# S4 convolution and SwiGLU on one core: half of the spectra paired by VectorE, the direct term on VectorE, block 1's halves kept on chip

## The chip, the core and the metric

The kernel runs on one core of one Trainium2 chip. The core has TensorE (matrix products into PSUM), VectorE, ScalarE and GpSimd (elementwise work; GpSimd also issues one kind of transfer) and SyncE, which issues most transfers here. Each engine works through its own instructions in a fixed order and waits for others at semaphores. The metric is the device time of one execution in microseconds (us), median of the runs. A profile is one further execution.

## The reference

Four residual layers on `x` of 2048 rows (L) by 512 columns (D): an S4 convolution, a SwiGLU, and both again with the same weights.

```python
dt = jnp.exp(log_dt)[:, None]
logdA = dt * A                      # A complex, D x N, N = 128
P = jnp.exp(logdA[:, :, None] * l)  # l = 0..2047
K = jnp.einsum("dn,dnl,dn->dl", Cc, P, dB).real
y = irfft(rfft(u, 2 * L) * rfft(K, 2 * L))[:L] + u * Dskip
...
x = x + A_ref(layernorm(x)); x = x + B_ref(layernorm(x))   # twice
B_ref(x) = (silu(x @ w_gate) * (x @ w_up)) @ w_down
```

K has 2048 lags for each of the 512 columns, and does not depend on x, so the kernel makes it once and uses it in both convolution layers.

## The kernel before

Two stages follow one another. The first, up to about 340 us, **builds** the spectra of K; the second runs the convolutions and the SwiGLU. The change is in the first.

The build runs over 8 chunks (`NCH`) of 64 columns (`DC`), and chunk c's steps are spread over two periods. In the order of data:

- **Tables of chunk c + 2** (`gen_turns`, `gen_exp`, `gen_trig`): VectorE makes phases in `im` (lines 386, 390 and the four doublings of line 394), ScalarE turns them into sines and cosines (lines 406 to 408) and makes the powers (line 421).
- **Factors of chunk c + 1** (`gen_g`, `gen_e`): VectorE multiplies them up (lines 441 to 448 into `re` and `im`; lines 455 to 483 into `g`, where the last half of `g` is completed by a 1 MB adding transfer that GpSimd issues, line 473).
- **Lags** (`lags`, lines 493 and 494): 128 small TensorE products from `g`, `re` and `im` give the chunk's 2048 x 64 lags in PSUM, `pk`. They need the last of VectorE's factors (line 448).
- **Spread** (`spread_in`, `spread`): ScalarE copies `pk` to `ks` (line 504); SyncE stores it to DRAM (`kdr`, line 511) and loads it back in another arrangement with four transfers (`kt`, line 513). For chunk 6 TensorE rearranges it instead (line 520), with a ScalarE copy (line 522).
- **Direct term** (`skip`, line 500): `Dskip` is added to lag 0, one row of `kt`, 1 x 64 elements. GpSimd does it for chunks 0 to 6; chunk 7's is VectorE's.
- **Spectra** (`spectra`): TensorE multiplies `kt` by the Fourier matrices (line 528) into `pw` in PSUM, for the frequency residues `q0` and `q0 + 2`: a call with q0 = 0 for chunks 0 to 6 and one with q0 = 1 for chunks 0 to 5, the latter a period later. The result W for three block offsets is the sum of two halves, one of block k and one, with a sign and real and imaginary parts exchanged, of block k - 1. ScalarE copies one half to `wo` (for q0 = 1 to a part of `spare`), line 552, the other to `wa`, line 554, and block 0 to `w0r`, line 555. SyncE stores `wo` to DRAM (`wdr`, line 535), and GpSimd then issues adding transfers of `wa` onto the same places (line 535 too, called from line 561): the pairing is done by the transfers. `wa` has one buffer.
- **Block 1's direct transform** (`second`, `direct`, lines 302 and 290): a half h and a residue q per chunk. SyncE loads the half's 512 rows from DRAM (`ndr`) into two buffers of the tag `uu` (line 306; the tag has three), TensorE transforms them (line 296), ScalarE copies the result (line 299), and SyncE stores it (line 300). Four residues use the same half, and each loads it again.
- **Norms of the weights** (`norms`): GpSimd loads weight tiles (line 324), ScalarE squares them (line 330), TensorE sums the squares (line 333), VectorE takes the largest (line 336).

The order of the work in the build is written out by hand: each step is put into `plan` with a time (`at(t, step)`), the plan is sorted, and every engine's instructions follow that sequence. The times are only keys of the order; when something runs is settled by the semaphores. `use(c, t)` puts chunk c's steps, `prepare` the tables, `factors` the factors. In the second stage the order is made by a scheduler that simulates the program; a change of the build can therefore move instructions there too.

Of the kernel before, what the change touches and what calls it, by code (L numbers as in the profile page):

```python
# [15 lines left out]
AF = mybir.ActivationFunctionType  # L16
OP = mybir.AluOpType
# [5 lines left out]
P = 128  # L23
T = 512
NB = L // T
FT = 11
FR = F % P
HD = D // 2
# [6 lines left out]
DC = 64  # L35
# [39 lines left out]
def kernel(ctx, tc, x, a_re, a_im, b_re, b_im, c_re, c_im, log_dt, d_skip,  # L75
                           w_gate, w_up, w_down, c_ef, c_ei, c_ek, c_am, c_eh, c_eih, out):
    nc = tc.nc
    V, A, G, PE = nc.vector, nc.scalar, nc.gpsimd, nc.tensor
# [9 lines left out]
    def tl(shape, name, tag, dt=F32):  # L88
        return sb.tile(shape, dt, name=name, tag=tag, bufs=BUFS[tag])
# [58 lines left out]
    ndr = dram.tile([2, 2, P, 2, HD], F32, name="ndr")  # L148
# [141 lines left out]
    def direct(b, h, q, n, space=psml):  # L290

        pf = space([P, 2, HD], "pf")
        for i in range(2):
            for c in range(4):
                e = ek[q // 2][:, q % 2, c - 1, i] if c else ef[:, q, i]
                PE.matmul(pf[:, i], lhsT=e, rhs=n[c], start=c == 0, stop=c == 3)
        yield
        u = tl([P, NQ, 2, DC], "u", "uu")
        A.activation(parted(u), whole(pf), AF.Copy)
        nc.sync.dma_start(udr[0][b, h, q], u)  # L300

    def second(h, q, space=psml):
        n = []
        for cp in range(2):
            t = tl([P, 2, HD], "n1", "uu")
            nc.sync.dma_start(t, ndr[h, cp])
            n += [t[:, 0], t[:, 1]]
        return direct(1, h, q, n, space)


    def norms():
# [185 lines left out]
    def skip(ch, kt, eng):  # L497

        k = kt[0:1, :, 0]
        eng.tensor_tensor(k, k, dsk[:, ch * DC:(ch + 1) * DC].rearrange("p (g d) -> p g d", g=4), OP.add)  # L500
# [33 lines left out]
    def store_w(h, c, q, wo, eng=nc.sync, **add):  # L534
        eng.dma_start(wdr[1:, h, q, :, c].rearrange("k p i d -> p k (i d)"), wo.rearrange("p k i d -> p k (i d)"), **add)

    def spectra(ch, kt, q0):


        h, cq = ch // NQ, ch % NQ  # L540
        pw = pbig([P, 2, 2, NB, 4, 16], "pw")
        for j in range(2):
            products(pw[:, j], kt, 0, NB, q0 + 2 * j, [(i, c) for i in range(2) for c in range(4)])
        yield
        if q0:
            wo = spare[0][:, 16 * DC:].rearrange("p (j k i d) -> p j k i d", j=2, k=NB - 1, i=2)
        else:
            wo = tl([P, 2, NB - 1, 2, DC], "wo", "sg")
        wa = tl([P, 2, NB - 1, 2, DC], "wa", "z")
        pv = pw.rearrange("p j i k g d -> p i j k (g d)")  # L550
        for i, sign in signs(q0):
            A.activation(wo[:, :, :, i], pv[:, 1 - i, :, :NB - 1], AF.Copy, scale=sign)
        for i in range(2):
            A.activation(wa[:, :, :, i], pv[:, i, :, 1:], AF.Copy)
        A.activation(w0r[:, h, q0::2, cq], pw[:, :, :, 0].rearrange("p j i g d -> p j i (g d)"), AF.Copy)
        yield
        for j in range(2):
            store_w(h, cq, q0 + 2 * j, wo[:, j])
        yield
        for j in range(2):  # L560
            store_w(h, cq, q0 + 2 * j, wa[:, j], G, accum_op=OP.add)
        yield

    def first_parts(c0, q):

# [376 lines left out]
    with tc.manual_schedule(engines={mybir.EngineType.Activation, mybir.EngineType.DVE, mybir.EngineType.PE, mybir.EngineType.Pool}):  # L942
# [57 lines left out]
        def at(t, f, n=1):  # L1000
            plan.append((t, len(plan), (lambda: take(f, n)) if hasattr(f, "__next__") else f))
# [5 lines left out]
        def prepare(c, t):  # L1007

            def tiles():
                ts[c] = gen_tiles(c)  # L1010
            at(t + 0.05, tiles)
            steps = {k: later(lambda g=g: g(c, ts[c])) for k, g in
                     (("turns", gen_turns), ("exp", gen_exp))}
            tr = later(lambda: gen_trig(ts[c]))
            at(t + 0.35, steps["turns"])
            at(t + 0.45, tr)
            at(t + 13.0, steps["turns"], 6)
            at(t + 17.0, tr)
            at(t + 8.3, steps["exp"], 100)

# [19 lines left out]
        def use(c, t):  # L1040

            box, kt, n = {}, kt2[:, c % 2], starts[c + 1]

            def copy():
                box["ks"] = spread_in(box["pk"])
                if c < NCH - 2:
                    spread(c, box["ks"], kt)
            at(t, lambda: box.update(pk=lags(ts[c], gs[c])))
            at(t + 7.1, copy)
            if c == NCH - 2:  # L1050
                at(t + 10.0, lambda: spread_pe(box["ks"], kt))
            at(t + 12.5, lambda: skip(c, kt, G))
            at(t + 25.0, lambda: sizes(c, kt, box["ks"]))
            for q0, ats in list(enumerate(((t + 17.5, t + 25.2, n + 2.1, n + 7.5),
                                      (n + 6.9, n + 14.0, n + 17.3, n + 21.0))))[:2 if c < NCH - 2 else 1]:
                sp = later(lambda q0=q0: spectra(c, kt, q0))
                for t0 in ats:
                    at(t0, sp)
# [26 lines left out]
        for i in range(NCH - 1):  # L1085
            t = starts[i]
# [12 lines left out]
        t = starts[NCH - 1]  # L1099
# [8 lines left out]
        c, kts, tail = NCH - 1, (kt2[:, 0], kt2[:, 1]), {}  # L1108
# [149 lines left out]
```

## Time and profile before

| | |
|---|---|
| median of 3 runs | 1203.43 us (1202.81 to 1205.57) |
| the profiled execution | 1196.63 us |
| its span, first to last instruction | 1194.8 us |
| its mean TensorE clock | 0.981 of full |
| busy over the span: TensorE, VectorE, ScalarE, GpSimd | 93%, 83%, 50%, 11% |
| moved by transfers | 156.28 MB in 134643 packets |

In the lines of the profile, PE is TensorE, PEld its weight loads, DVE VectorE, ACT ScalarE, POOL GpSimd, SP SyncE; a "q" behind a name is that engine's sequencer, which issues transfers and waits. L500 is line 500 of the kernel before. A timeline row has the start, the duration (both us), the engine, the line, the operation, output<-input, and the shapes; in brackets stands how long the engine was idle before it and what ended that. Names keep no buffer numbers.

### The profile page before, as it was taken

The page shows a single profiled execution, that of the slowest core. Times are in us where ns is not written, and L with a number is a line of the kernel's source. Part 1 is how long each engine was busy: PE and PEld are TensorE (multiplying, and loading weights), DVE is VectorE, ACT ScalarE, POOL GpSimd, SP SyncE. Part 2 cuts the span into 40 slices and gives each one's busy share as a digit, 9 for nine tenths or more (in the row PEclk, how much of TensorE's full clock was granted, in tenths as well). Part 3 has the DMA queues.
Part 4 walks back from the last instruction along what each step waited for, and adds up shares of the span by engine and source line. Part 5 has one row for each costly group of instructions (what it writes and reads, how often), then busy time and mean ns, then how long its engine had stood idle before and what let it go on. Part 6 is the DMA issues. An engine that isn't in the chain of part 4 may idle for free.

```text
span 1194.8 us, 24454 instructions
## 1 busy us (share of the span) xinstructions
PE 1109.1 (93%) x9948; PEld 880.3 (74%) x9948; DVE 995.7 (83%) x1579; ACT 600.0 (50%) x1208; POOL 132.7 (11%) x183
## 2 busy tenths in 40 slices
PE   1889978898799998999999999989999999999998
PEld 1768867787687676878777686858687786867875
DVE  7999988874888999999899999989996799983211
ACT  6789778833272444447644252664532552325211
POOL 0013333331000010000100000121100010000000
PEclk9989988999899999999999999999999999999999
DMA  5359887879475326433334454433435145312000
GB/s 202 132 149 219 188 165 162 190 178 249 138 228 163 121 101 203 138 120 81 102 96 155 119 163 153 117 90 110 127 124 184 34 121 140 112 58 45 14 23 18
DMA packets 134643, 156.28 MB, mean 131 GB/s; under 512 B 51313, under 2 KB 81777, under 8 KB 134530
## 3 DMA queue, kind: packets, MB, share of 16 engines
q1 hardware_dynamic: 117026, 126.47, 34.4%
q0 software_dynamic: 17504, 28.25, 11.6%
q8 instruction: 78, 1.28, 0.4%
q14 instruction: 35, 0.29, 0.1%
HBM read 101.85 MB, written 36.57 MB: 116 GB/s over the span
## 4 chain that ended last, share of the span: by engine, by line
PE 33%; DVE 22%; issue 9%; DMA 6%; POOL 1%; SPq 1%; ACT 1%; DVEq 0%; POOLq 0%; ACTq 0%
PE pgu L900 5%; PE pgu L901 5%; PE pgu L903 5%; DVE t L767 3%; PE py L915 3%; PE py L916 3%; PE py L917 3%; DVE yk L770 3%; PE pi L787 2%; DVE yk L767 2%; DMA mix<-nn 2%; DVE z L228 2%; PE pf L280 2%; DVE sg L907 1%; DMA w<-wdr 1%
## 5 line engine op out<-in xcount | busy, mean ns | idle before, releaser
L900 PE MATMUL pgu<-mix,wsl 128*128 128x256 f16 x1280 | 298.4, 272 | 5.8 <-DVE xg L920 3.5
L901 PE MATMUL pgu<-mix,wsl 128*128 128x256 f16 x1280 | 298.5, 273 | 0.0
L903 PE MATMUL pgu<-mix,wsl 128*128 128x256 f16 x1280 | 194.8, 273 | 0.0
L901 PEld LDWEIGHTS <-wsl 128*128 128x128 f16 x1280 | 125.2, 98 | 22.8 <-issue 6.9
L915 PE MATMUL py<-wsl,hh 128*128 128x512 f16 (+1 forms) x352 | 134.8, 383 | 6.9 <-DVE xg L920 6.4
L900 PEld LDWEIGHTS <-wsl 128*128 128x128 f16 x1280 | 125.2, 98 | 15.7
L903 PEld LDWEIGHTS <-wsl 128*128 128x128 f16 x1280 | 125.2, 98 | 14.6
L917 PE MATMUL py<-wsl,hl 128*128 128x512 f16 (+1 forms) x352 | 134.7, 383 | 1.0 <-DVE hl L909 1.0
L916 PE MATMUL py<-wsl,hh 128*128 128x512 f16 x320 | 122.7, 383 | 0.0
L767 DVE TENSOR_TENSOR t<-uu,w 128x1024 f32<-128x1024 f32 x96 | 117.1, 1220 | 4.9 <-DMA w<-wdr 4.2
L770 DVE TENSOR_TENSOR yk<-yk,t 128x1024 f32<-128x1024 f32 x96 | 117.1, 1220 | 0.2
L906 ACT ACTIVATE sg<-pgu,sc 128x512 f32<-128x512 f32 x80 | 54.6, 682 | 119.4 <-PE pgu L903 116.2
L907 DVE SCALAR_TENSOR_TENSOR sg<-pgu,sc,sg 128x512 f32<-128x512 f32 x80 | 59.8, 747 | 54.4 <-ACT sg L906 54.3
L528 PE MATMUL pw<-kt,ek 128*128 128x256 f32 (+1 forms) x384 | 96.7, 391 | 0.0
L908 ACT ACTIVATE hh<-sg 128x512 f16<-128x512 f32 x80 | 50.1, 626 | 79.7 <-DVE sg L907 79.7
L528 PEld LDWEIGHTS pw<-kt,ek 128*128 128x128 f32 x384 | 77.1, 205 | 10.5
L787 PE MATMUL pi<-yl,mix 128*128 128x256 f16 x576 | 78.8, 272 | 3.5 <-DVE yl L228 3.3
L280 PE MATMUL pf<-z,eh 128*128 128x256 f16 x576 | 74.9, 273 | 0.1
L767 DVE TENSOR_TENSOR yk<-u,w0r 128x1024 f32<-128x1024 f32 x56 | 68.3, 1220 | 2.8 <-ACT u L282 2.6
L916 PEld LDWEIGHTS <-hh 128*128 128x128 f16 (+1 forms) x352 | 34.7, 99 | 44.5 <-issue 9.4
L909 DVE TENSOR_TENSOR hl<-sg,hh 128x512 f16<-128x512 f32 x80 | 55.0, 688 | 14.8 <-ACT hh L908 14.8
L493 PE MATMUL pk<-re,g 128*32 128x64 f32 x1024 | 61.5, 301 | 5.5 <-DVE re L448 3.3
(237 smaller groups left out, 2186.7 us busy)
## 6 DMA issues: line engine op xcount, KB each, us to landing
w<-wdr SPq DMA_DIRECT2D x96, 256.0 KB, 2.7
uu<-udr SPq DMA_DIRECT2D x96, 256.0 KB, 2.9
udr<-u POOLq DMA_DIRECT2D x32, 256.0 KB, 2.4
g<-g POOLq DMA_DIRECT2D x6, 1024.0 KB, 9.8
wdr<-wa POOLq DMA_DIRECT2D x26, 192.0 KB, 7.0
udr<-u SPq DMA_DIRECT2D x16, 256.0 KB, 3.0
n<-ndr SPq DMA_DIRECT2D x16, 256.0 KB, 4.6
n<-xdr SPq DMA_DIRECT2D x4, 1024.0 KB, 5.7
```

The source lines that it names most:

```text
L280: PE.matmul(pf[:, o], lhsT=e, rhs=m, start=k == 0, stop=k == len(terms) - 1)
L528: PE.matmul(pw[:, i], lhsT=e, rhs=kt[:, :, c + 4 * k0:4 * k1:4, :].rearrange("p g k d -> p k g d"), start=c == 0, stop=c == 3)
L767: V.tensor_tensor(t, uu.unsqueeze(2).to_broadcast([P, NQ, 2, 2, DC]), w.unsqueeze(3).to_broadcast([P, NQ, 2, 2, DC]), OP.mult)
L770: V.tensor_tensor(yk, yk, t, OP.add)
L787: PE.matmul(pi[:, o], lhsT=e, rhs=m, start=k == 0, stop=k == len(terms) - 1)
L900: PE.matmul(o, lhsT=wgu(wi, k, 0)[:, fs], rhs=nh[:, k], start=k == 0, stop=False)
L901: PE.matmul(o, lhsT=wgu(wi, k, 1)[:, fs], rhs=nh[:, k], start=False, stop=False)
L903: PE.matmul(o, lhsT=wgu(wi, k, 0)[:, fs], rhs=nlo[:, k], start=False, stop=k == 3)
L907: V.scalar_tensor_tensor(sg, pgu[:, 1], sc6[:, 4:5], sg, OP.mult, OP.mult)
L915: PE.matmul(py[:, r], lhsT=hh[:n, f, rc], rhs=wd(f, 0)[:n], start=f == 0, stop=False)
L916: PE.matmul(py[:, r], lhsT=hh[:n, f, rc], rhs=wd(f, 1)[:n], start=False, stop=False)
L917: PE.matmul(py[:, r], lhsT=hl[:n, f, rc], rhs=wd(f, 0)[:n], start=False, stop=f == FT - 1)
```

## The change

It has three parts, and a small shift of the order.

- In `spectra`, the calls with q0 = 0 no longer copy the second half to `wa`. VectorE adds it, straight out of PSUM, onto `wo` in place, and SyncE stores the finished sum. The adding transfers remain for q0 = 1.
- `skip` runs on VectorE for all chunks, and stands between the second and the third doubling of the phases (the doublings are split 3 and 3 for it).
- `second` loads a half of block 1 once and keeps its two tiles for the four residues that use it: 4 loads in place of 16. Two of the three buffers of `uu` are taken meanwhile.

```diff
+    halves = {}
+
     def second(h, q, space=psml):
-        n = []
-        for cp in range(2):
-            t = tl([P, 2, HD], "n1", "uu")
-            nc.sync.dma_start(t, ndr[h, cp])
-            n += [t[:, 0], t[:, 1]]
-        return direct(1, h, q, n, space)
+        if h not in halves:
+            halves[h] = n = []
+            for cp in range(2):
+                t = tl([P, 2, HD], "n1", "uu")
+                nc.sync.dma_start(t, ndr[h, cp])
+                n += [t[:, 0], t[:, 1]]
+        return direct(1, h, q, halves[h], space)
...
-        wa = tl([P, 2, NB - 1, 2, DC], "wa", "z")
         pv = pw.rearrange("p j i k g d -> p i j k (g d)")
         for i, sign in signs(q0):
             A.activation(wo[:, :, :, i], pv[:, 1 - i, :, :NB - 1], AF.Copy, scale=sign)
-        for i in range(2):
-            A.activation(wa[:, :, :, i], pv[:, i, :, 1:], AF.Copy)
+        if q0:
+            wa = tl([P, 2, NB - 1, 2, DC], "wa", "z")
+            for i in range(2):
+                A.activation(wa[:, :, :, i], pv[:, i, :, 1:], AF.Copy)
         A.activation(w0r[:, h, q0::2, cq], pw[:, :, :, 0].rearrange("p j i g d -> p j i (g d)"), AF.Copy)
         yield
+        if not q0:
+            wv = wo.rearrange("p j k i d -> p i j k d")
+            V.tensor_tensor(wv, pv[:, :, :, 1:], wv, OP.add)
+            yield
         for j in range(2):
             store_w(h, cq, q0 + 2 * j, wo[:, j])
         yield
-        for j in range(2):
-            store_w(h, cq, q0 + 2 * j, wa[:, j], G, accum_op=OP.add)
-        yield
+        if q0:
+            for j in range(2):
+                store_w(h, cq, q0 + 2 * j, wa[:, j], G, accum_op=OP.add)
+            yield
...
-            at(t + 13.0, steps["turns"], 6)
+            at(t + 13.0, steps["turns"], 3)
+            at(t + 13.2, steps["turns"], 3)
...
-            at(t + 12.5, lambda: skip(c, kt, G))
+            at(t + 13.1, lambda: skip(c, kt, V))
```

What the orders look like at three places, taken from chunk 3's period (line numbers behind each L are those of the kernel that the rows are from; the changed kernel's are 3 to 9 higher).

On VectorE, the place between the factors `g` of one chunk and the factors `re` and `im` of the same chunk, with the doublings of a later chunk's phases between. Before:

```order
L390 TENSOR_TENSOR im<-tdk,am 128x128
L394 ISA im<-im 128x256
L394 ISA im<-im 128x512
L394 ISA im<-im 128x1024
L394 ISA im<-im 128x2048
L443 TENSOR_TENSOR re<-re 128x2048
L445 SCALAR_TENSOR_TENSOR im<-im,mu 128x1984
L448 TENSOR_TENSOR re<-re,mu 128x124x8 x2
```

And in the changed kernel:

```order
L393 TENSOR_TENSOR im<-tdk,am 128x128
L397 ISA im<-im 128x256
L397 ISA im<-im 128x512
L503 TENSOR_TENSOR kt_438<-kt_438,tdk 1x4x16
L397 ISA im<-im 128x1024
L397 ISA im<-im 128x2048
L446 TENSOR_TENSOR re<-re 128x2048
L448 SCALAR_TENSOR_TENSOR im<-im,mu 128x1984
L451 TENSOR_TENSOR re<-re,mu 128x124x8 x2
```

The direct term has come in between the doublings, and everything below it on VectorE now stands behind a wait for `kt`.

On VectorE again, some instructions later, where the next factors `g` begin; the changed kernel alone (before, the row of `wo` is not there):

```order
L458 TENSOR_TENSOR xz<-xz,mz_156 128x960
L462 TENSOR_TENSOR g<-w_152,re 128x2x64
L463 TENSOR_TENSOR spare<-w_152,im 128x2x64
L444 TENSOR_TENSOR im<-im,re 128x2048
L389 TENSOR_TENSOR xz<-th,am 128x320
L563 TENSOR_TENSOR wo<-pw,wo 128x2x6x64
L465 TENSOR_TENSOR g<-g,spare 128x64
L466 TENSOR_TENSOR g<-g,spare 128x64
```

The pairing of q0 = 0, 768 elements a partition, is a new instruction there. It waits for ScalarE's copies to `wo`.

On GpSimd, one period, before:

```order
L396 MEMSET im 128x64
L324 DMA st<-in_B_w_gate_dram 128x344 x3
L535 DMA wdr<-wa 128x3x128 x2
L324 DMA st<-in_B_w_gate_dram 128x344 x2
L535 DMA wdr<-wa 128x3x128 x2
L419 MEMSET re 128x64
L473 DMA g<-g 128x2x1024
L500 TENSOR_TENSOR kt_438<-kt_438,tdk 1x4x16
```

And in the changed kernel:

```order
L399 MEMSET im 128x64
L327 DMA st<-in_B_w_gate_dram 128x344 x3
L538 DMA wdr<-wa 128x3x128 x2
L327 DMA st<-in_B_w_gate_dram 128x344
L327 DMA st<-in_B_w_up_dram 128x344
L422 MEMSET re 128x64
L476 DMA g<-g 128x2x1024
L399 MEMSET im 128x64
```

One of the two pairs of adding transfers and the direct term are gone from the period.

## The prediction

> **What bounds the kernel now.** I read the page first, then the build in windows from one direct term to the next, then the timelines of the engines around the places where the windows differ. The page gives the span and the busy tenths of TensorE, VectorE and the DMA engines in 40 slices of 29.9 us:
>
> ```profile
> span 1194.8 us, 24454 instructions
> ...
> PE   1889978898799998999999999989999999999998
> ...
> DVE  7999988874888999999899999989996799983211
> ...
> DMA  5359887879475326433334454433435145312000
> ```
>
> The build is slices 0 to 11. In slices 1 to 4 VectorE is full, in 5 to 8 it is not, though the same work is repeated chunk by chunk, and the transfers are heavy throughout. From slice 12 on TensorE is full. The windows run from the direct term of one chunk to that of the next (length, PE, PEld, DVE, ACT, POOL, clock, DMA share):
>
> ```profile
> 78.70:104.90 26.20, 25.31 (x332) 22.22 (x333) 25.75 (x31) 24.12 (x55) 7.74 (x13) 0.93 0.83 198
> 104.90:132.40 27.50, 27.50 (x346) 24.36 (x345) 27.05 (x32) 25.30 (x56) 10.99 (x16) 1.00 0.91 199
> 132.40:169.90 37.50, 31.04 (x350) 25.65 (x348) 35.24 (x38) 29.12 (x64) 9.88 (x14) 0.91 0.87 174
> 169.90:200.90 31.00, 28.34 (x341) 24.72 (x341) 21.95 (x28) 24.73 (x56) 9.96 (x14) 0.94 0.84 171
> 200.90:233.40 32.50, 28.76 (x342) 24.73 (x342) 30.64 (x34) 25.39 (x58) 11.68 (x14) 0.89 0.87 183
> 233.40:262.50 29.10, 27.37 (x360) 23.36 (x361) 21.02 (x25) 12.99 (x18) 9.11 (x13) 0.94 0.81 190
> ```
>
> Two regimes: 26.2 and 27.5 us, with VectorE busy 98% of it, then 37.5, then 29 to 32.5 with VectorE at 71 to 94%. ScalarE's timeline shows what came between them:
>
> ```profile
> 89.13 0.89 ACT L552 ACTIVATE wo<-pw 128x384 f32<-128x384 f32 x2
> ...
> 142.38 0.87 ACT L552 ACTIVATE wo<-pw 128x384 f32<-128x384 f32 x2
> 151.49 0.87 ACT L554 ACTIVATE wa<-pw 128x384 f32<-128x384 f32 x2 [8.23 <-DMA wdr<-wa]
> ...
> 157.09 1.00 ACT L504 ACTIVATE ks<-pk 128x1024 f32<-128x1024 f32 x1
> ```
>
> ScalarE stood for 8.23 us, because the one buffer of `wa` was still being added to DRAM, and `ks`, on which the next chunk's spread hangs, is behind it in order. GpSimd's timeline shows why that was late, and what happened to the direct term afterwards:
>
> ```profile
> 78.73 0.80 POOL L500 TENSOR_TENSOR kt<-kt,tdk 1x64 f32<-1x64 f32 x1
> ...
> 140.91 1.30 POOL L535 DMA_DIRECT2D wdr<-wa  x1 [5.62 <-DMA wdr<-spare]
> ...
> 157.88 2.33 POOL L473 DMA_DIRECT2D g<-g  x1
> 169.85 0.31 POOL L500 TENSOR_TENSOR kt<-kt,tdk 1x64 f32<-1x64 f32 x1 [9.64 <-DMA kt<-kdr]
> ...
> 262.48 1.86 POOL L500 TENSOR_TENSOR kt<-kt,tdk 1x64 f32<-1x64 f32 x1 [9.26 <-ACT kt L522]
> ```
>
> The adding transfers of q0 = 1 had to wait for the plain stores before them; those of q0 = 0 shared their buffer half a period later. From then on VectorE ran ahead of the spread: the 1 MB `g<-g` goes out before the four `kt` loads instead of after them. The transfers of the window 96 to 108 and of the window 156 to 172 (KB each, median us to landing) show the price:
>
> ```profile
> kdr<-ks SPq DMA_DIRECT2D x1, 512.0 KB, 4.4
> kt<-kdr SPq DMA_DIRECT2D x4, 128.0 KB, 2.9
> ```
>
> ```profile
> kt<-kdr SPq DMA_DIRECT2D x4, 128.0 KB, 7.0
> wdr<-spare SPq DMA_DIRECT2D x2, 192.0 KB, 4.7
> ```
>
> `kt` takes 7.0 us in place of 2.9, the direct term waits 9.64 us for it, and the spectra wait for the direct term. So the late build is a loop through the spread, and the early build is VectorE's own work. From the direct term at 78.73 to that at 262.48 six laps take 183.75 us.
>
> **The change part by part.** VectorE's timeline gives the laps without a spread in the way, and the place of the new wait:
>
> ```profile
> 77.88 2.74 DVE L394 CUSTOM_DVE_ANT_0 im<-im 128x256 uint16<-128x256 uint16 x4
> ...
> 91.16 0.22 DVE L462 TENSOR_TENSOR g<-g,spare 128x64 f32<-128x64 f32 x1
> ...
> 104.11 2.74 DVE L394 CUSTOM_DVE_ANT_0 im<-im 128x256 uint16<-128x256 uint16 x4
> ...
> 111.70 2.29 DVE L448 TENSOR_TENSOR re<-re,mu 128x992 f32<-128x992 f32 x2
> ...
> 131.04 2.74 DVE L394 CUSTOM_DVE_ANT_0 im<-im 128x256 uint16<-128x256 uint16 x4
> ...
> 222.79 2.74 DVE L394 CUSTOM_DVE_ANT_0 im<-im 128x256 uint16<-128x256 uint16 x4
> ...
> 237.29 0.29 DVE L459 TENSOR_TENSOR g<-w,re 128x128 f32<-128x128 f32 x1 [4.15 <-ACT re L408]
> ...
> 255.46 2.28 DVE L443 TENSOR_TENSOR re<-re 128x2048 f32<-128x2048 f32 x1
> ```
>
> Laps: 104.11 - 77.88 = 26.2 and 131.04 - 104.11 = 26.9, the second with a reduction (line 336) in it; mean 26.6. The last one, to chunk 6's place, is 255.46 - 222.79 - 4.15 idle = 28.5. What VectorE gets on top is priced by its rows grouped by line and shape (mean ns last but one):
>
> ```profile
> L748 DVE TENSOR_TENSOR bb<-bb,pi 128x512 f32<-128x512 f32 x4 | 2.7, 686 | 0.1
> ...
> L591 DVE TENSOR_TENSOR wos<-pw,wos 128x384 f32<-128x384 f32 x4 | 2.2, 555 | 4.0 <-ACT wos L590 4.0
> ...
> L500 DVE TENSOR_TENSOR kt<-kt,tdk 1x64 f32<-1x64 f32 x1 | 0.2, 214 | 9.9 <-issue 9.9
> ```
>
> The pairing adds 768 elements out of PSUM: between 0.69 (512 elements) and 2 x 0.555 = 1.11; along the line through both rows, 1.02 ns an element, 0.686 + 256 x 0.00102 = 0.95. The direct term is 0.21. Together 1.2 us a lap.
>
> So laps that VectorE sets would take 26.6 + 1.2 = 27.8, five of them 139.0, and the sixth 28.5 + 1.2 = 29.7; sum 168.7 against 183.75, a gain of 15.
>
> Does the spread still fit, now that VectorE waits for it in order? Count from the direct term S. The doublings left, lines 443, 336, 445 and 448 end at 111.70 + 2.29 = 113.99, 9.1 us after 104.85 (104.11 and the first two of the four doublings, an estimated 0.7 of the 2.74 by their share of the elements and a fixed part each). TensorE's spectra meanwhile take 113.9 - 107.05, about 7, when they are not held up:
>
> ```profile
> 79.59 1.22 PE L528 MATMUL pw<-kt,ef 128*128 128x256 f32 x2 [2.00 <-POOL kt L500]
> ...
> 107.05 0.59 PE L528 MATMUL pw<-kt,ef 128*128 128x256 f32 x2
> ...
> 112.66 1.46 PE L528 MATMUL pw<-kt,ek 128*128 128x256 f32 x6
> ```
>
> They hide in the 9.1. Then the lags, by the first and last starts in two laps, and the issue of the `kt` loads:
>
> ```profile
> L493 PE MATMUL pk<-re,g x128: 287/287/302, 88.1 to 94.9; 128*32 128x64 f32 x128
> L493 PE MATMUL pk<-re,g x128: 268/287/318, 142.1 to 151.2; 128*32 128x64 f32 x128
> ```
>
> ```profile
> 101.48 1.75 SPq L513 DMA_DIRECT2D kt<-kdr  x4
> ```
>
> The lags take 7 to 9.3 us with the last products; I take 7.5, nearer the first, since the second fell into the lap that was disturbed; `ks` 1.0 and a start-up of 0.2; `kdr` 4.4; the fourth `kt` load leaves 1.3 after the first (three of four issues in 1.75) and lands 2.9 later. S + 0.2 + 9.1 + 7.5 + 1.2 + 4.4 + 1.3 + 2.9 = S + 26.6, against VectorE's next arrival at S + 27.8: it fits by 1.2 us, and `g<-g`, issued 0.9 us before the direct term, again follows `kt`. That margin is thin, and carries the forecast.
>
> What is taken away: 14 of 26 copies to `wa` (13 calls, two each; 0.87 a pair: 6 us of ScalarE in all, so `ks` is reached no later), 14 adding transfers of 192 KB and 12 loads of 256 KB, 2.8 + 3.1 = 5.8 MB. In 184 us at about 185 GB/s some 34 MB move, so a sixth less contention; I count nothing for it. The 8.23 us stand of ScalarE goes, since `wa` is then used once a lap and has 27 us to land. What waits anew: VectorE for `wo`. ScalarE had it done at 89.13 + 0.89 = 90.02 in chunk 0, 11.3 after its direct term, and VectorE comes to the place ahead of line 462 at 91.16; hidden by 1.1 us, and the two copies that ScalarE no longer makes stood behind, not before. The store of `wo` moves behind the next `kt` loads on SyncE; it has 11 us to land before ScalarE writes `wo` again, where the store of `spare`, of the same size, took 4.7 in the full lap. GpSimd has less to do. The kept halves cost nothing while the third `uu` buffer turns over once a lap. After the build the distance from chunk 6's direct term to the second stage hangs on `kt`, `pk` and loads that all follow it, so I move it as a whole; block 1's last transform, with no load of its own now, may add 0 to 4 us. The scheduler's other order in the second stage I price at 0, between -3 and +3.
>
> Sum: 1196.63 - 15 = 1181.6 for an execution like the profiled one. The three timed runs lie 6.8 us above that one, so I give 1203.43 - 15 = 1188.4.
>
> **A rule weighed.** At 79.59 TensorE had stood 2.00 us, and the next two products took 1.22 us, where the pair at 107.05, with no wait before it, took 0.59. The Trainium skill, "TensorE: Matmul & The Clock Gate", says under "What's actually happening" that an idle window of about 3.4 us drops the array to half rate. The new wait before the lags leaves TensorE about 9.1 - 7 = 2.1 us idle each lap; by the rule that is under a window and may cost nothing, by the row it can cost some. By the row's way the loss lands in the spectra's 2.1 us of cover; it decides only where the margin of 1.2 us is gone, which is the last rival.
>
> **The rivals.**
> (a) Part of the gain is given back. The second stage is TensorE's, full in its slices, so a build that ends earlier should move everything, but a reordered stage or longer norms of the weights before the last lags (they wait for loads that GpSimd issues) could eat half: 1203.4 - 8 = 1195.
> (b) The spread stays contended. VectorE comes to the direct term first, `g<-g` is out, `kt` takes 7.0: a lap is 26.6 + 4.1 = 30.7, six 184.2, and the time stays at 1203.4 + 0.5 = 1204. For it: every lap after 169.85. Against it: VectorE can no longer run ahead, as its own wait holds back the next `g<-g`.
> (c) Slower: the wait in VectorE's order. It decides once `kt` lands more than 27.8 us after S. With `kt` at 7.0 and lags at a lowered clock, 9.3 instead of 7.5 as from 142.1 to 151.2, a lap is 30.7 + 1.8 = 32.5, six 195, 11 more than now: 1214. For it: the thin margin and the clocks of 0.89 to 0.94 above. That the parts don't do what they say is ruled out by the order: 4 loads of `ndr`, 12 copies to `wa`.
>
> **How the numbers follow.** Forecast 0.57, (a) 0.16, (b) 0.10, (c) 0.17. Within 0.2%, 2.4 us, counts as no change, about what a measurement can tell here. Faster is the forecast and (a), 0.73; the same is (b), 0.10; slower is (c), 0.17. The forecast's own range is 1181 (the 4 us of the last transform and 3 of the order) to 1194 (the pairing at 1.11 in seven laps, 1 us; +3 of the order; 1 us lost in two laps). The range that holds the time 8 times in 10 reaches to (b): 1181 to 1204.
>
> **What would show it.** Right: VectorE's direct terms 27 to 28.5 us apart from chunk 0 to 5, with idle time before them under 1 us; `kt` landing in about 3 us in all chunks; no wait of ScalarE for `wdr<-wa`; the pairing at 0.9 to 1.0 us; chunk 6's direct term near 247; the first product of the second stage (line 900 before) some 15 us earlier. Wrong: idle time before line 503 of several us a lap, with `kt` at 5 or more; ScalarE's copies to `wo` late; or a build that ends early and a span that doesn't.

## The result and the profile after

The changed kernel took 1166.3 us, median of four executions (1163.68 to 1168.48), beside 1203.94 us before (1202.81 to 1205.57): a ratio of 0.9685, 95% interval 0.9662 to 0.9709. The gain is 37.6 us; 15 were forecast, and the time lies below the range of 1181 to 1204. In the experiments the time before varied from 1194.0 to 1205.9 us between executions; two of the experimental kernels scatter by 2% as well, the ratio there leaves out the executions far from the fastest, and I read their single times.

The page of the changed kernel, span and busy tenths as shown of before (slices of 29.0 us):

```profile
span 1161.5 us, 24413 instructions
...
PE   1979999998889999999999999999999999999998
...
DVE  7999999978889999999899999989994999983212
...
DMA  5356777766493437332254454342534145312000
```

VectorE is now full up to slice 7, where it had fallen off from slice 5 on. The windows from one direct term to the next, chunks 0 to 6 (length, PE, PEld, DVE, ACT, POOL, clock, DMA share, GB/s):

```profile
78.67:105.76 27.09, 26.83 (x334) 23.39 (x335) 26.68 (x34) 24.44 (x55) 4.82 (x10) 0.91 0.60 156
105.76:133.59 27.83, 27.78 (x348) 24.56 (x347) 27.42 (x34) 25.38 (x57) 7.54 (x12) 1.00 0.78 182
133.59:160.69 27.10, 26.25 (x346) 22.82 (x344) 26.69 (x34) 23.67 (x54) 7.01 (x11) 1.00 0.72 165
160.69:188.29 27.60, 25.50 (x334) 22.67 (x334) 27.19 (x34) 24.08 (x54) 7.00 (x11) 1.00 0.73 167
188.29:215.80 27.51, 27.44 (x352) 24.04 (x350) 27.10 (x35) 24.54 (x57) 7.52 (x12) 1.00 0.85 202
215.80:244.28 28.48, 27.05 (x367) 23.20 (x366) 28.03 (x33) 16.46 (x20) 6.80 (x10) 1.00 0.75 177
```

All six laps are VectorE's (98% busy), 165.6 us in sum where before had 183.8. VectorE's prices, grouped by line and shape (us in all, mean ns of one, idle time before them):

```profile
L563 DVE TENSOR_TENSOR wo<-pw,wo 128x768 f32<-128x768 f32 x7 | 6.7, 961 | 0.2 <-ACT w0r L559 0.2
...
L503 DVE TENSOR_TENSOR kt<-kt,tdk 1x64 f32<-1x64 f32 x8 | 1.6, 206 | 8.5 <-ACT kt L525 8.5
```

Every wait of ScalarE from 78 to 262 us (engine, line, waited for: us in total, times, longest):

```profile
ACT re L409 <- DVE im L397: 16.1, 6, 3.8
ACT ks L507 <- PE pk L497: 10.4, 5, 6.6
ACT kt L525 <- PE kp L523: 7.9, 1, 7.9
ACT sq L333 <- DMA st<-in_B_w_up_dram: 4.1, 3, 1.9
```

The pairing costs 0.96 us and waits 0.2 us in all; the direct term waits only in chunk 7. ScalarE no longer waits for `wdr<-wa`; in the same view of before it did:

```profile
ACT wa L554 <- DMA wdr<-wa: 10.0, 3, 8.2
```

The build up to chunk 6's direct term makes 18.2 us of the gain, and the second stage 10.6. Between the two profiled executions (spans 1194.8 and 1161.5 us):

| stretch | before | after | difference |
|---|---|---|---|
| start to chunk 6's direct term | 262.5 | 244.3 | -18.2 |
| chunk 6's to chunk 7's direct term | 24.4 | 21.6 | -2.9 |
| from there to the first FFN product, block 1's last transform not counted | 51.3 | 49.7 | -1.6 |
| second stage, that transform (3.5 us) counted in both | 856.6 | 846.0 | -10.6 |

That transform stands behind the first FFN products before, and ahead of them after. The second stage, the same work product for product, is 10.6 us shorter. TensorE's waits in it before, the five largest (columns as for ScalarE):

```profile
PE py L915 <- DVE xg L920: 6.4, 5, 3.2
PE pgu L900 <- DVE xg L920: 3.5, 3, 1.2
PE pi L787 <- DVE yl L228: 3.3, 4, 1.5
PE pgu L867 <- DMA mix<-nn: 2.5, 1, 2.5
PE pgu L900 <- DVE sg L907: 2.3, 3, 2.0
```

The same view of the changed kernel, with its two largest rows and the two that fell most besides `xg`:

```profile
PE pgu L909 <- DVE sg L916: 4.6, 2, 4.3
PE py L924 <- DVE xg L929: 3.0, 5, 0.8
...
PE pgu L878 <- DMA mix<-nn: 0.4, 1, 0.4
PE pi L796 <- DVE yl L228: 0.3, 1, 0.3
```

All rows of the two views add up to 21 and 12 us. Most are waits for VectorE, which by windows of 100 us is 83 to 100% busy in the first 700 us of this stage: what TensorE waits for is a place in VectorE's order. The longest wait for a residual add before, on VectorE's timeline:

```profile
790.27 1.22 DVE L767 TENSOR_TENSOR t<-uu,w 128x1024 f32<-128x1024 f32 x1
791.40 0.42 DVE L228 SCALAR_TENSOR_TENSOR xf<-t,xf 128x256 f32<-128x256 f32 x1
791.74 0.42 DVE L228 SCALAR_TENSOR_TENSOR t<-bb 128x256 f32<-128x256 f32 x1
792.07 0.75 DVE L228 SCALAR_TENSOR_TENSOR bb<-pi,sy,bb 128x512 f32<-128x512 f32 x1
792.73 1.22 DVE L767 TENSOR_TENSOR yk<-u,w0r 128x1024 f32<-128x1024 f32 x1
793.87 0.75 DVE L920 SCALAR_TENSOR_TENSOR xg<-py,sc,xg 128x512 f32<-128x512 f32 x1
```

and on TensorE's (idle time before it and its releaser in brackets):

```profile
794.66 0.38 PE L915 MATMUL py<-wsl,hh 128*128 128x512 f16 x1 [3.24 <-DVE xg L920]
```

The residual add at 793.87 frees the PSUM that the next `py` products need; five convolution operations, with no gap between them, stand in front of it, and TensorE stands 3.24 us.

### The profile page after: what moved, and what is told of

It is laid out like the page before. It is cut to its first block, busy times and chain, and to the rows that moved or that the text cites. A ratio compares the mean times of both kernels' runs of the same rounds, so it can differ in the third digit from the quotient of the medians.

```text
span 1161.5 us, 24413 instructions
## 1 busy us (share of the span) xinstructions
PE 1099.4 (95%) x9948; PEld 875.2 (75%) x9948; DVE 1000.5 (86%) x1593; ACT 594.4 (51%) x1194; POOL 109.1 (9%) x162
## 4 chain that ended last, share of the span: by engine, by line
PE 33%; DVE 26%; issue 8%; DMA 4%; ACT 3%; SPq 1%; POOL 1%; DVEq 0%; ACTq 0%; POOLq 0%
PE pgu L909 6%; PE pgu L910 5%; PE pgu L912 5%; DVE t L776 4%; DVE yk L779 4%; PE py L924 3%; PE py L925 3%; PE py L926 3%; DVE yk L776 3%; DVE z L228 2%; PE pi L796 2%; PE pf L280 2%; DVE sg L916 2%; DVE hl L918 1%; DMA mix<-nn 1%
## 5 line engine op out<-in xcount | busy, mean ns | idle before, releaser
L531 PE MATMUL pw<-kt,ek 128*128 128x256 f32 (+1 forms) x384 | 91.0, 374 | 0.0
L531 PEld LDWEIGHTS pw<-kt,ek 128*128 128x128 f32 x384 | 72.5, 193 | 8.6
```

The source lines that it names most:

```text
L531: PE.matmul(pw[:, i], lhsT=e, rhs=kt[:, :, c + 4 * k0:4 * k1:4, :].rearrange("p g k d -> p k g d"), start=c == 0, stop=c == 3)
```

## The experiments

Twelve kernels ran, each timed against the kernel before on the same chip. "Second stage" is the stretch from the first FFN product to the end. Where the last transform stands ahead of it, as in the kernels with the kept halves, its 3.5 us are to be added before such a figure is set beside one of the others; the table below does so.

**The parts one by one.** The theory was that the buffer of `wa` held the build (in the expectations, the order theory); the rivals were that the transfers' bytes did (the bytes theory), and that the second stage gains because the build ends earlier (the shift theory). First the pairing alone:

```diff
-        wa = tl([P, 2, NB - 1, 2, DC], "wa", "z")
...
+        if not q0:
+            wv = wo.rearrange("p j k i d -> p i j k d")
+            V.tensor_tensor(wv, pv[:, :, :, 1:], wv, OP.add)
```

> Before plus the pairing of q0 = 0 alone; the direct term stays on GpSimd, the halves are loaded each time. Order theory (the build gains because ScalarE's 8.2 us stand and the late spread go; the second stage gains only through the kept halves): direct term of chunk 6 at 245 to 250 us instead of 262.5, no wait of ScalarE for adding transfers above 1 us, second stage (first line-900 product to the end) within 4 us of before's 856.6, total 1184 to 1192. Bytes theory (the gain follows the bytes taken off the DMA engines, 2.8 of 5.8 MB here): half of the build's 18 us, direct term near 253, total about 1193. Shift theory (the second stage gains because the build ends earlier): second stage shorter by 5 to 10 us, total about 1178.

Measured: 1178.03 us (1176.31 to 1184.61), ratio 0.9815 [0.9779, 0.9851]. Laps 27.1, 27.8, 27.1, 27.6, 27.5, 27.5; chunk 6's direct term at 242.9; second stage 861.1. The pairing alone brings the whole gain of the build and none of the second stage's. The time is the 1178 of the shift theory, but by chance: its shorter second stage did not come, and the build gained more than the order theory had it.

The direct term alone:

```diff
-            at(t + 13.0, steps["turns"], 6)
+            at(t + 13.0, steps["turns"], 3)
+            at(t + 13.2, steps["turns"], 3)
...
-            at(t + 12.5, lambda: skip(c, kt, G))
+            at(t + 13.1, lambda: skip(c, kt, V))
```

> Before plus the direct term on VectorE alone, between the second and third doubling. Order theory: the adding transfers of q0 = 0 still share the buffer, so ScalarE stands 5 to 9 us once or more; VectorE now waits in order, so it stands at the direct term in that lap, and the lap behind is not one of 31 us but 27 to 28: build 5 to 12 us shorter, total 1190 to 1200. Bytes theory: no bytes are removed, no change, 1203. The wait in VectorE's order as a price: laps of 30 us and more, total above 1206.

Measured: 1202.93 us (ten executions), ratio 1.0009 [0.9987, 1.0032]; chunk 6's direct term at 269.9. ScalarE's wait for the buffer in its build:

```profile
ACT wa L554 <- DMA wdr<-wa: 15.4, 2, 7.7
```

and VectorE's wait for `kt`:

```profile
DVE kt L500 <- DMA kt<-kdr: 24.6, 5, 12.6
```

The late `kt` is still there, and now it is VectorE that stands for it. Moving a waiting instruction to another engine moved the wait and gained nothing, where 1190 to 1200 had been expected. The laps from chunk 0's direct term on are 27.9, 37.1, 27.1, 39.4, 27.3 and 32.4 us: VectorE's wait holds it back for one lap at a time, not for good.

The kept halves alone:

```diff
-        n = []
+        if h not in halves:
+            halves[h] = n = []
...
-        return direct(1, h, q, n, space)
+        return direct(1, h, q, halves[h], space)
```

> Before plus the kept halves alone. Its second stage has the same order on TensorE and VectorE as the changed kernel's; its build has before's pairing and direct term. Order theory: direct term of chunk 6 at 258 to 264, ScalarE's stand still there, second stage 8 to 12 us shorter than before's 856.6, total 1191 to 1196. Bytes theory: 3.1 of 5.8 MB go, half of the build's 18 us, direct term near 253, total about 1194 with a second stage as before. Shift theory: build and second stage as before, 1203.

Measured: 1186.3 us (1184.47 to 1188.78), ratio 0.9875 [0.9849, 0.9901]. The build is as long as before (chunk 6's direct term at 263.4), and the second stage is 843.1 us. ScalarE's stand for the buffer, which was expected to stay, is not there (from 78 to 262 us, where it was 10.0 us before):

```profile
ACT wa L557 <- DMA wdr<-wa: 0.6, 2, 0.4
```

Yet the laps are 28.0, 35.7, 30.1, 31.0, 31.9 and 27.4 us, and GpSimd's direct terms of chunks 2 to 5 wait 8.4 to 8.9 us each for `kt`. So a long build does not need the stand for `wa`.

The build gives nothing, and 843.1 + 3.5 stand against 856.6: twelve loads less in the build, and 10 us gained after it. The ratio makes it 14; the other 4 are the distance of before's profiled execution, 1196.63, to the median on this chip, 1200.65. The product of this ratio and the pairing's is 0.969, the whole change.

Pairing and direct term together:

```diff
+            V.tensor_tensor(wv, pv[:, :, :, 1:], wv, OP.add)
...
+            at(t + 13.1, lambda: skip(c, kt, V))
```

> The changed kernel without the kept halves: pairing and direct term on VectorE, 16 loads of the halves. Its second stage has the same order as the pairing alone. Order theory: laps of 27 to 28 us as in the changed kernel, direct term of chunk 6 at 244 to 247, second stage within 4 us of 856.6, total 1180 to 1186. Bytes theory: half the gain, direct term near 253. Shift theory: second stage 8 to 12 us shorter, total 1166 to 1172.

Measured: 1176.86 us (1174.96 to 1177.16), ratio 0.9792 [0.9768, 0.9815]; second stage 855.8. Beside the pairing the direct term is again worth nothing that can be told.

**What is it in the kept halves?** The last of the eight transforms is the only one that the second stage sees. Loading its half afresh:

```diff
-        if h not in halves:
+        if h not in halves or (h, q) == sec[-1]:
```

> The changed kernel, with one thing undone: the last of block 1's eight transforms loads its half afresh (two loads of 256 KB); the other kept halves stay. If the gain of the second stage hangs on that last transform, which then stands 90 products behind the first FFN product instead of ahead of it and brings another order of VectorE and TensorE with it, the build stays (chunk 6's direct term at 244) and the second stage goes from 842.5 back to 855 to 861 us: 1174 to 1180. If it hangs on the loads saved in the build, ten of twelve are still saved and the time stays near 1166 to 1168.

Measured: 1175.59 us (1174.71 to 1176.32), ratio 0.9788 [0.9759, 0.9817]; second stage 855.2. Two loads put back, and the gain of the second stage is gone; ten loads are still saved. Then all loads kept, and only the last two issued earlier:

```diff
+        early = half(sec[-1][0])
         odd = later_parts(c - 1, kts[0], (3, 1))
...
-        take(second(*sec[-1]), 2)
+        take(second(*sec[-1], n=early), 2)
```

> The kernel with the pairing and the direct term on VectorE (1176.9), no kept halves, so all sixteen loads are made; only the two loads of the last transform are issued earlier, ahead of the products of the last chunk. The transform then stands ahead of the first FFN product, and the second stage has the same order as in the changed kernel. If the place of the last transform is the cause, this has the whole gain without any kept half: second stage 842 to 846, 1164 to 1169. If it takes the kept halves themselves, it stays at 1175 to 1179.

Measured: 1165.78 us (1165.7 to 1167.3), ratio 0.9706 [0.9672, 0.974]; second stage 843.6. No half is kept, and all of the gain is there. In this kernel the rows of TensorE and VectorE in the second stage are those of the changed kernel, one for one. Is it the early transform, or the order that the scheduler made with it? The same early transform, emitted one step sooner:

```diff
+        take(second(*sec[-1]), 2)
         sizes(c, kts[1], ks)
         direct_size()
         nn2 = tl([P, 2, D], "nn2", "nn")
-        take(second(*sec[-1]), 2)
```

> The changed kernel, with the last transform emitted one step earlier, ahead of the two reductions for the sizes instead of behind them. It still stands ahead of the first FFN product, but the scheduler then gives the second stage another order: on VectorE some 0.69 like the changed kernel's and 0.79 like that of the kernels with a late transform. If it is the early transform that carries the gain, whatever the order, the second stage is 841 to 847 and the time 1164 to 1170. If it is the particular order that the scheduler happens to give, the second stage can land anywhere between 843 and 861, and if it keeps nothing of the gain the time is 1174 to 1180.

Measured: 1177.34 us (1175.91 to 1180.39), ratio 0.9806 [0.9773, 0.9839]; second stage 854.8, with the transform ahead of the first FFN product (320.9) as in the change. So it is the order: with 3.5 added, this stage is 858.3, as long as with a late transform. TensorE's waits of this kernel in the second stage:

```profile
PE py L924 <- DVE xg L929: 8.6, 7, 3.0
PE pgu L909 <- DVE sg L916: 5.6, 4, 3.2
PE pgu L878 <- DMA mix<-nn: 1.8, 1, 1.8
```

All rows of this view add up to 23 us, 21 before. How full VectorE is in the first 200 us of the stage shows which kind of order it is. This kernel, in windows of 100 us:

```profile
320.90:420.90 100.00, 92.13 (x750) 73.35 (x749) 88.14 (x155) 47.31 (x94) 5.16 (x7) 1.00 0.52 163
420.90:520.90 100.00, 95.27 (x795) 72.65 (x794) 96.01 (x158) 46.90 (x91) 8.49 (x13) 0.98 0.52 145
```

The changed kernel, likewise:

```profile
319.00:419.00 100.00, 95.50 (x766) 76.20 (x765) 94.00 (x166) 48.12 (x94) 7.34 (x9) 0.97 0.55 170
419.00:519.00 100.00, 98.07 (x832) 75.74 (x830) 99.44 (x169) 49.50 (x97) 8.16 (x12) 1.00 0.48 151
```

With the transform one step sooner VectorE does 9 us less in these 200 us and has to do it later, and TensorE is 6 us behind after 200 us already. That the work put off is what TensorE later waits for is argued, not shown row by row.

Last, the change without its direct term, and without its pairing:

```diff
-            at(t + 13.1, lambda: skip(c, kt, V))
+            at(t + 12.5, lambda: skip(c, kt, G))
```

> The changed kernel without its second part: the direct term stays on GpSimd, pairing and kept halves are as in the change, and the second stage has the changed kernel's order. If moving the direct term is worth nothing either way (alone it measured 1.0009, beside the pairing 1176.9 against 1178.0), the time is 1163 to 1168 and the second stage 842 to 845. If VectorE's 0.2 us a lap count, it is 1 to 2 us faster than the change; if GpSimd's direct term is late beside the pairing, it is 2 or more slower.

Measured: 1166.45 us (1165.07 to 1168.04), ratio 0.9724 [0.9683, 0.9765]; second stage 844.4. It equals the changed kernel.

```diff
-            V.tensor_tensor(wv, pv[:, :, :, 1:], wv, OP.add)
...
+        for i in range(2):
+            A.activation(wa[:, :, :, i], pv[:, i, :, 1:], AF.Copy)
```

> The changed kernel without its first part, the pairing: direct term on VectorE and kept halves. The build should be that of the run with the direct term alone, contended, with chunk 6's direct term at 260 to 272. The scheduler gives the second stage an order of its own, on VectorE 0.93 like the changed kernel's. If what matters is to be near that order, the second stage is 842 to 847 us and the time 1184 to 1192; if each order is a draw of its own, it can be anything up to 860 and the time up to 1204.

Measured: 1186.08 us (1185.57 to 1187.22), ratio 0.9889 [0.9855, 0.9923]; chunk 6's direct term at 265.6, second stage 841.8, in an order of its own that is near the changed kernel's. All second stages by order, the last transform counted in:

| order of the second stage | kernels | us |
|---|---|---|
| before's | before; no pairing (below) | 856.6; 857.8 |
| with the pairing or the direct term | pairing; direct term; both; traffic kept (below); last loaded; hold only (below) | 861.1; 857.5; 855.8; 859.3; 855.2; 858.0 |
| transform one step sooner | other order | 858.3 |
| with the kept halves | change; halves; loaded early; direct on GpSimd | 846.0; 846.6; 847.1; 847.9 |
| direct term and halves | that kernel | 845.3 |

Within one order the spread is at most 6 us, whatever the build; the means of the second and the fourth row are 11 us apart. Two orders are good and three are not, and nothing in the edits says which. TensorE's waits do: in the five kernels of the last two rows they add up to 12 to 14 us in this stage, in the nine others to 20 to 24, and VectorE is busy for 191 to 193 us of its first 200 in the five, for 183 to 187 in the nine.

**What held the build?** The pairing takes away two things at once, the second filling of `wa` and half of the adding transfers. Here, beside the kernel with the pairing alone, the transfers go out as before, from a table that nothing writes:

```diff
-        if q0:
-            for j in range(2):
-                store_w(h, cq, q0 + 2 * j, wa[:, j], G, accum_op=OP.add)
+        for j in range(2):
+            src = wa[:, j] if q0 else ef.rearrange("p q i f -> p (q i f)")[:, :384].rearrange("p (k i d) -> p k i d", k=NB - 1, i=2)
+            store_w(h, cq, q0 + 2 * j, src, G, accum_op=OP.add)
```

> The kernel before with the pairing of q0 = 0 on VectorE, as in the run with the pairing alone (1178.0), but the two adding transfers of q0 = 0 still go out from GpSimd at their old place, with the same bytes to the same addresses, from a constant that nothing writes; so a constant is added to those spectra. The transfers are those of before, while the one buffer of `wa` is filled once a lap instead of twice. If the build was held by ScalarE's wait for that buffer, the laps stay at 27 to 28 us, ScalarE shows no wait for wdr<-wa, chunk 6's direct term comes near 243, and the time is 1175 to 1182. If it was held by the transfers themselves (their bytes, their adding, GpSimd's issues), the laps go back to 29 to 37, chunk 6's direct term comes at 255 or later, and the time is 1190 or more.

Measured: 1179.64 us (1178.71 to 1180.95), ratio 0.9823 [0.9793, 0.9853]; laps 27.4, 27.5, 27.1, 27.7, 27.5, 27.5. The transfers were not the cause. They do cost margin, though. Take the lap that begins at 134.47 here and at 133.59 in the change. SyncE's issues of the `kt` loads with the traffic kept:

```profile
156.76 1.76 SPq L513 DMA_DIRECT2D kt<-kdr  x4
```

with these landings in that lap (KB each, median us):

```profile
kdr<-ks SPq DMA_DIRECT2D x1, 512.0 KB, 4.2
kt<-kdr SPq DMA_DIRECT2D x4, 128.0 KB, 3.3
```

In the changed kernel the issues are

```profile
153.65 1.74 SPq L516 DMA_DIRECT2D kt<-kdr  x4
```

and the landings

```profile
kdr<-ks SPq DMA_DIRECT2D x1, 512.0 KB, 2.6
kt<-kdr SPq DMA_DIRECT2D x4, 128.0 KB, 2.9
```

With 1.3 us to the fourth issue, `kt` is there 26.9 us after the direct term with the traffic kept, and 24.3 us after it in the change; with the pairing alone, which differs from the first in these transfers, it is 24.9. VectorE's lap is 27.1 in all three.

Then, beside the kernel before, neither pairing nor second filling, with all transfers:

```diff
-        for i in range(2):
-            A.activation(wa[:, :, :, i], pv[:, i, :, 1:], AF.Copy)
+        if q0:
+            wa = tl([P, 2, NB - 1, 2, DC], "wa", "z")
+            for i in range(2):
+                A.activation(wa[:, :, :, i], pv[:, i, :, 1:], AF.Copy)
...
-            store_w(h, cq, q0 + 2 * j, wa[:, j], G, accum_op=OP.add)
+            src = wa[:, j] if q0 else ef.rearrange("p q i f -> p (q i f)")[:, :384].rearrange("p (k i d) -> p k i d", k=NB - 1, i=2)
+            store_w(h, cq, q0 + 2 * j, src, G, accum_op=OP.add)
```

> The kernel before with GpSimd's direct term, all loads and all adding transfers, and without any pairing on VectorE; only ScalarE's two copies of q0 = 0 into `wa` are left out, and its adding transfers send a constant in their place (so those spectra are wrong by what was not added). The one buffer of `wa` is thus filled once a lap, and VectorE has no new wait. The second stage has the order of before. If the wait for that buffer alone held the build, the laps are VectorE's own without the 0.95 of the pairing, 26 to 27 us in place of 27.1 to 27.8, chunk 6's direct term comes at 236 to 242, and the time is 1172 to 1180. If the build needed VectorE held back by the pairing, so that it cannot run ahead of the spread (g<-g before the kt loads), laps of 29 us and more come back, with chunk 6's direct term at 250 or later and a time of 1188 or more.

Measured: 1174.73, 1200.45, 1185.93 and 1195.63 us; ratio 0.984 [0.9765, 0.9914]. The execution with a profile is the fastest, with laps of 27.0, 26.2, 26.4, 27.1, 26.6 and 28.4 and chunk 6's direct term at 240.4. So a free buffer lets VectorE run at its own pace, but does not keep it there. Either the wait in VectorE's order or the slower pace must be what keeps it. In the kernel with the traffic kept, one element in place of 768:

```diff
-            V.tensor_tensor(wv, pv[:, :, :, 1:], wv, OP.add)
+            V.tensor_tensor(wv[:, 0, 0, 0, :1], pv[:, 0, 0, 1, :1], wv[:, 0, 0, 0, :1], OP.add)
```

> The kernel of the run with the traffic kept (1179.6, all four executions within 1178.7 to 1181.0), with one thing changed: VectorE's addition at the pairing's place is of one element per partition instead of 768, so it still waits for ScalarE's `wo` and PSUM in the same place of VectorE's order, but costs some 0.06 us instead of 0.95. The spectra of q0 = 0 are wrong, as there. Without any such instruction the executions ran from 1174.7 to 1200.5. If it is the wait in VectorE's order that keeps the build out of the contended laps, this is steady: all executions within 3 us, laps 26.2 to 27.3, 0.9 us a lap faster than with the traffic kept, 1172 to 1177. If it is the slower pace, which gives the spread chain (an estimated 26.6 us) its slack, the executions scatter again, some of them at 1185 to 1200.

Measured: 1190.8, 1185.23, 1185.79, 1193.31, 1177.84 and 1173.71 us; ratio 0.9824 [0.9785, 0.9864]. The wait is there, the 0.95 us have become 0.16 (0.06 was expected), and the executions scatter over 20 us where the kernel with the full pairing kept within 2.2. GpSimd's timeline around two direct terms, with the traffic kept:

```profile
105.88 1.19 POOL L473 DMA_DIRECT2D g<-g  x1 [7.39 <-DVE im L390]
106.95 0.51 POOL L500 TENSOR_TENSOR kt<-kt,tdk 1x64 f32<-1x64 f32 x1
...
133.71 1.19 POOL L473 DMA_DIRECT2D g<-g  x1 [7.43 <-DVE im L390]
134.47 0.84 POOL L500 TENSOR_TENSOR kt<-kt,tdk 1x64 f32<-1x64 f32 x1
```

and with the one element, in a profiled execution of 1190.8 us:

```profile
104.38 1.19 POOL L473 DMA_DIRECT2D g<-g  x1 [6.28 <-DVE im L390]
106.59 0.64 POOL L500 TENSOR_TENSOR kt<-kt,tdk 1x64 f32<-1x64 f32 x1 [1.02 <-DMA kt<-kdr]
...
132.10 1.19 POOL L473 DMA_DIRECT2D g<-g  x1 [5.67 <-DVE im L390]
134.62 0.33 POOL L500 TENSOR_TENSOR kt<-kt,tdk 1x64 f32<-1x64 f32 x1 [1.33 <-DMA kt<-kdr]
```

In the first, `kt` has landed when GpSimd comes to the direct term after issuing `g<-g`; in the second it waits 1.02 and 1.33 us for it, and the next lap is 32.0 us. So with the traffic kept it is the pairing's own 0.95 us a lap that keeps VectorE behind the spread. Whether a delay of another kind and the same length would do it was not tried.

## Why the prediction was wrong

**The step that failed** is the one on the second stage: "The scheduler's other order in the second stage I price at 0, between -3 and +3." It was worth 10.6 us between the profiled executions (1176.86 against 1166.3 between the medians without and with the kept halves), and the same early transform in another order gives it back. The prediction counted TensorE "full in its slices" and moved the stage as a block. But TensorE stood some 21 us in it, 18 of them for a VectorE that was itself 83 to 100% busy, and the order decides how much of that. A bound of 3 us had no row behind it; TensorE's waits in the stage, 21 us, would have been the bound on the side of a gain.

The order alone does not make the miss: without it the time is 1176.9 (pairing and direct term alone), still below the range. Of the 22 us between the forecast of 1188.4 and the 1166.3 measured, the order made 10.6, the laps 3.1, the two stretches behind them 2.9 and 1.6, where the prediction moved this distance "as a whole" and allowed 0 to 4 us on top, and the offset from the profiled execution to the median 4.2.

**The build's mechanism was right, its size a little small.** The laps became VectorE's, as said: 165.6 us against "sum 168.7". The lap with nothing added is 26.2 to 27.1 (no pairing), where 26.6 was taken; the pairing, forecast at 0.95, measured 0.96, and the direct term 0.21. "27.8" for each of the first five was still 0.4 too much (mean 27.4), and the last was 28.5 instead of 29.7. ScalarE's wait went, as said, but a build without it can be as long as before: the kernel with the kept halves has the long laps and 0.6 us of that wait. And what the prediction named to keep VectorE from running ahead, "its own wait holds back the next `g<-g`", is not what does it: with the pairing alone, where VectorE waits for no `kt` up to chunk 6, the laps are the same, and with the direct term alone long laps came back after each short one. With all transfers in place it was the pairing's 0.95 us, which the prediction counted in the lap that the spread had to fit, but not as what keeps VectorE back. So that the laps came out right was in part luck.

**The offset did not carry over.** "The three timed runs lie 6.8 us above that one, so I give 1203.43 - 15" took the distance between the profiled execution of before and its median for a constant. In the changed kernel it is 2.6 us. With pairing and direct term alone the median fell by 24 us (1200.65 to 1176.86), and the executions of that kernel lie within 2.2 us. That the scatter of before is made in its contended laps fits the runs without the pairing's pace, which scatter likewise; no slower execution of before has a trace, so it is argued, not shown.

**The margin.** "That margin is thin, and carries the forecast" was right in what decides, and wrong in the numbers that it was put together from: "a sixth less contention; I count nothing for it" left out that `kdr<-ks` can then land in 2.6 us instead of 4.4, which makes most of the way from the S + 26.6 forecast to S + 24.3 in the lap shown. With the traffic kept it is S + 26.9, close to the forecast, and there the 0.95 us decide: with them 1178.7 to 1181.0, without them 1173.7 to 1193.3. Something like rival (b), the contended spread, is what the kernels without that pace do in most executions.

**Rival (a)** foresaw that a reordered stage could matter, but only as a loss; (c) did not come, as `kt` landed in 2.9 us in the median. "May add 0 to 4 us" for the last transform: the stretch up to the first FFN product, less that transform, became 1.6 us shorter.

**The rule weighed** was not put to the test in the laps: TensorE's longest stand between chunks 0 and 6 is 1.3 us, and the clock granted is 1.00 in five of the six laps. The window of about 3.4 us that the Trainium skill gives under "TensorE: Matmul & The Clock Gate", "What's actually happening", is never reached there. Just ahead of the laps it is reached, and the trace agrees with it; the row that was set against it was misread. Before, the granted clock was 0.50 already from 76 to 82 us, ahead of the stand of 2.00 us, and TensorE had stood 3.47 us up to 75.97. In the change it had stood 3.49 us up to 76.01, the clock was 0.50 from 77 to 83 us, which is the 0.91 of the first lap, and the same two products took 1.22 us behind a stand of only 1.29. So no price of a 2 us stand can be read from that row.

**Open:** whether the pace alone, with `wa` still filled twice a lap, would do; whether the change, with half of the transfers gone, still needs the pace; why the stretches behind chunk 6's direct term became 4.5 us shorter; why stages of one and the same order differ by up to 6 us; and what a scheduler would have to aim at to find the better orders. No kernel measured here is below the changed one by more than its scatter; the kernel with the two loads issued earlier (1165.8) and the one with the direct term on GpSimd (1166.5) equal it with less change.

## What to carry to other kernels

Where a scheduler orders a stage, an edit far ahead of it can change the order, and what can be gained is what the bounding engine waits in that stage, not zero: read those waits before pricing an order, and keep a good order by hand once one is found. When two chains run a lap with a margin near nothing, slowing the one that runs ahead can be the gain, and a scatter between executions can be a sign of such a margin. Test an edit's parts singly: here one of three carried the build, one the second stage by way of the order alone, and one nothing.

## What was not expected of the hardware

Fewer transfers in flight shortened others. With a mean DMA share of 0.72 in place of 0.95 in the lap shown, the 512 KB store `kdr<-ks` landed in 2.6 instead of 4.2 us (3.0 with the pairing alone, at 0.81), while the four 128 KB loads behind it took 2.9 instead of 3.3. The mean share of a lap does not foretell it, though: in the changed kernel's first lap, at 0.60, that store took 4.3 us. The transfers of `wdr` in the changed kernel (KB each, median us from issue to landing):

```profile
wdr<-wo SPq DMA_DIRECT2D x14, 192.0 KB, 2.9
...
wdr<-spare SPq DMA_DIRECT2D x12, 192.0 KB, 2.6
wdr<-wa POOLq DMA_DIRECT2D x12, 192.0 KB, 9.9
```

An adding transfer took more than three times the time of a plain store of the same size to land here. Before, with 26 of them, it was 7.0 us beside 3.5 for `wo` and 4.7 for `spare`.
